# Upward feed-forward products of a second pass, written as seven block products for eight

## The chip, the core and the metric

One core of one Trainium2 chip runs the whole kernel. The metric is device time in microseconds (us), the median of several runs. TensorE does the matrix products, VectorE and ScalarE work on 128 partitions side by side, GpSimd does one reduction, and SyncE starts nearly all DMA transfers.

## The reference

The inputs are float32. Four batches of twelve heads, 448 positions of 64 values, go through an attention with a capped score; the result x has 4 x 448 = 1792 rows of 768. Two feed-forward layers follow, and only the second one's result is returned.

```python
x = attention(q, k, v, cap)                  # (1792, 768): tanh cap, softmax, times v
h = np.maximum(x @ w_in, 0.0)                # w_in (768, 2048)
x = h * h @ w_out                            # (2048, 768)
g = x @ w_gate                               # w_gate, w_val (768, 1536)
x = g * (1 / (1 + np.exp(-g))) * (x @ w_val) @ w_out2    # (1536, 768)
```

## The kernel before

The 768 columns of x are six blocks of 128 (KD), kept transposed: one tile holds 128 columns of one batch by its 448 rows. The feed-forward work is cut into **units**. A "1a" unit makes 128 columns of h (six blocks of contraction), a "2a" unit 128 columns of the gate or of the value, a "1b" or "2b" unit adds four blocks (FG) of the hidden layer into 128 columns of the result. `units` (L398) lists them: for each group of four hidden blocks the upward units, then six downward ones, first for layer one (4 groups), then for layer two (3 groups). That is 16 "1a", 24 "1b", 24 "2a" and 18 "2b".

The batches go through this list in two passes: pass 0 takes batches 0 and 1 (with the attention of batches 2 and 3 fitted in between its units), pass 1 takes batches 2 and 3. In a pass each unit runs for one batch and then for the other.

Every product is made in three matmuls (`unit_mm`, L497; the matmul L508): a float32 operand is split into a rounded piece and what is left of it, and high x high, high x low and low x high are added up in PSUM. One contraction block therefore costs three matmuls of 128 x 128 by 448. Splitting a weight block costs a cast on ScalarE (`w_hi`, L482) and a subtraction on VectorE (`w_lo`, L487); the same holds for x (`x_hi`, L391, `x_lo`, L395) and for the hidden layer (`g_hi`, L543, `g_lo`, L547). What comes after an upward product is on ScalarE (relu L523, square L527, tanh of the gate L531) and VectorE (L535, L539); a downward product is added to the sum on VectorE (`gather`, L555; the first group is copied on ScalarE, L553). Results are transposed on VectorE (L560) and stored from SyncE's queue (L565).

Weights arrive as 64-bit floats and are decoded in pass 0 on VectorE (L464, L466, L468), and written to DRAM; pass 1 reads them from there (L442). The attention's rows of batches 2 and 3 lie in DRAM too (`hold`, L384) and come back at the start of pass 1, twelve loads of 224 KB (`x_back`, L388).

The order of all work is made by a planner, `Plan.order` (L38): each operation has an engine, an assumed duration, a rank (when it would be due) and a list of what it needs, and buffers go round in rings. It takes the operation that can start first, and among equals the one with the lowest rank. The result is one fixed order for each engine, and engines take their queues in that order. Constants such as PACE, AHEAD, LATER, SLACK and MARGIN (L137 to L152) only move ranks and assumed delays. The instructions of SyncE's queue, loads, stores and the write-back of decoded weights, are one such order.

Of the kernel before, what the change touches and what calls it, by code (L numbers as in the profile page):

```python
# [101 lines left out]
def kernel(  # L102
# [34 lines left out]
    FIRST = [15.0, 20.6]  # L137
    LAST = [80.7, 39.3]
    STRETCH = 1.8

    AHEAD = dict(
        ld=45.5, lv=27.5, tr=4.6, cp=3.2, sc=9.4, th=-3.9, top=-8.4, par=-2.5, mp=6.1, sub=16.3,
        ex=20.4, rs=-12.2, av=30.6, rc=15.3, norm=-4.5, xh=33.0, xl=30.4,
    )
    LATER = dict(
        ld=-22.4, lv=-11.1, tr=6.7, sc=-4.9, th=11.3, top=9.7, par=19.0, sub=25.6, ex=16.7,
        tot=26.9, av=11.0, rc=4.2, norm=-13.9, xh=27.9, xl=34.2,
    )
# [262 lines left out]
    passes = [([0, 1], units(0)), ([2, 3], units(0))]  # L411
# [246 lines left out]
    PAIR = 6.33  # L658
# [193 lines left out]
```

## Time and profile before

| | |
|---|---|
| median of 3 runs | 1242.69 us (1242.67 to 1242.75) |
| the profiled execution's own time | 1251.49 us |
| its span, first to last instruction | 1249.4 us |
| TensorE busy, share of the span | 98% |
| VectorE, ScalarE, GpSimd | 65%, 42%, 6% |
| mean granted TensorE clock | 0.996 of full speed |

The profile is of one execution. Busy times are sums over instructions, and idle time is put down to what ended it. Pass 0 with the attention lasts to 736 us of the span, pass 1 from there to 1243 us, and the last 6 us are the store of the result. The table's shares are means over both passes, so they must not be read as those of either.

### The profile page before, as it was taken

The page shows a single profiled execution, that of the slowest core. Times are in us where ns is not written, and L with a number is a line of the kernel's source. Part 1 is how long each engine was busy: PE and PEld are TensorE (multiplying, and loading weights), DVE is VectorE, ACT ScalarE, POOL GpSimd, SP SyncE. Part 2 cuts the span into 40 slices and gives each one's busy share as a digit, 9 for nine tenths or more (in the row PEclk, how much of TensorE's full clock was granted, in tenths as well). Part 3 has the DMA queues.
Part 4 walks back from the last instruction along what each step waited for, and adds up shares of the span by engine and source line. Part 5 has one row for each costly group of instructions (what it writes and reads, how often), then busy time and mean ns, then how long its engine had stood idle before and what let it go on. Part 6 is the DMA issues. An engine that isn't in the chain of part 4 may idle for free.

```text
span 1249.4 us, 16191 instructions
## 1 busy us (share of the span) xinstructions
PE 1229.2 (98%) x6292; PEld 999.8 (80%) x6292; DVE 814.4 (65%) x1261; ACT 528.4 (42%) x788; POOL 75.9 (6%) x31
## 2 busy tenths in 40 slices
PE   8989999999999999999999999999999999999997
PEld 5334477887887787788788889999999999999997
DVE  5999888878888988888898863133335432334334
ACT  5988754626354443534234335333334223221220
POOL 2222110100010000011001000000000000000000
PEclk9999999999999999999999999999999999999999
DMA  7352057365463664753664783111212112112004
GB/s 139 68 135 67 16 153 202 119 171 153 123 175 116 176 170 118 200 159 115 155 187 133 205 217 93 57 47 55 56 60 61 41 55 65 47 51 63 26 1 89
DMA packets 214428, 135.54 MB, mean 108 GB/s; under 512 B 144816, under 2 KB 193360, under 8 KB 214352
## 3 DMA queue, kind: packets, MB, share of 16 engines
q1 hardware_dynamic: 212496, 134.28, 39.6%
q8 instruction: 49, 0.80, 0.3%
q10 hardware_dynamic: 1856, 0.23, 0.1%
q14 instruction: 27, 0.22, 0.1%
HBM read 99.48 MB, written 35.00 MB: 108 GB/s over the span
## 4 chain that ended last, share of the span: by engine, by line
PE 89%; DVE 7%; DMA 2%; issue 1%; ACT 1%; POOL 0%; SPq 0%; DVEq 0%; ACTq 0%
PE ff L508 77%; PE av L345 5%; PE sc L259 5%; DVE mx L278 1%; PE rs L309 1%; DVE te L296 1%; DVE tt L296 1%; DVE x L395 1%; DMA out_dram<-ob 0%; PE rs L329 0%; DVE acc L555 0%; DMA wx<-w 0%; DVE wx L468 0%; DVE wx L466 0%; DVE wp L487 0%
## 5 line engine op out<-in xcount | busy, mean ns | idle before, releaser
L508 PE MATMUL ff<-x,wp 128*128 128x448 f32 x2880 | 600.9, 368 | 0.5 <-DVE x L395 0.5
L508 PEld LDWEIGHTS ff<-x,wp 128*128 128x128 f32 x2880 | 538.0, 188 | 69.2 <-issue 19.2
L508 PE MATMUL ff<-g,wp 128*128 128x448 f32 x2016 | 418.7, 367 | 0.0
L508 PEld LDWEIGHTS ff<-g,wp 128*128 128x128 f32 x2016 | 377.4, 188 | 43.3 <-issue 9.4
L482 ACT CAST wp<-wx 128x768 fp32r<-128x768 f32 (+1 forms) x164 | 118.5, 723 | 223.8 <-PE ff L508 112.7
L487 DVE TENSOR_TENSOR wp<-wx,wp 128x512 fp32r<-128x512 f32 (+1 forms) x164 | 134.2, 820 | 64.6 <-ACT wp L482 63.5
L547 DVE TENSOR_TENSOR g<-gg,g 128x448 fp32r<-128x448 f32 x112 | 70.2, 627 | 110.2 <-ACT g L543 109.9
L555 DVE TENSOR_TENSOR acc<-ff,acc 128x448 f32<-128x448 f32 x120 | 74.6, 622 | 76.3 <-PE ff L508 75.0
L283 POOL PARTITION_ALL_REDUCE mr<-mx x24 | 75.1, 3131 | 582.9 <-DVE mx L278 547.3
L543 ACT CAST g<-gg 128x448 fp32r<-128x448 f32 x112 | 63.4, 566 | 85.5 <-DVE gg L539 83.1
L259 PE MATMUL sc<-kT 64*112 64x448 f32 x384 | 88.6, 571 | 1.9 <-DVE xs L381 1.3
L535 DVE SCALAR_TENSOR_TENSOR sg<-th,ff 128x448 f32<-128x448 f32 x48 | 29.8, 620 | 76.7 <-ACT th L531 76.7
L300 ACT ACTIVATE tt<-tt,capt 112x896 f32<-112x896 f32 x60 | 62.5, 1045 | 23.4 <-DVE tt L296 23.2
L523 ACT ACTIVATE r<-ff 128x448 f32<-128x448 f32 x64 | 34.8, 544 | 87.8 <-PE ff L508 87.8
L531 ACT ACTIVATE th<-ff 128x448 f32<-128x448 f32 x48 | 26.2, 546 | 106.5 <-PE ff L508 106.2
L466 DVE SCALAR_TENSOR_TENSOR wx<-wr,wx 128x512 int32<-128x512 int32 (+1 forms) x82 | 68.5, 836 | 1.8
L468 DVE SCALAR_TENSOR_TENSOR wx<-wr,wx 128x512 int32<-128x512 int32 (+1 forms) x82 | 66.9, 816 | 1.1
L259 PEld LDWEIGHTS sc<-kT 64*112 64x112 f32 x384 | 31.5, 175 | 44.0 <-issue 26.3
L539 DVE SCALAR_TENSOR_TENSOR gg<-ff,sg 128x448 f32<-128x448 f32 x48 | 29.9, 624 | 51.6 <-PE ff L508 51.4
L272 ACT ACTIVATE tt<-sc,capt 112x896 f32<-112x896 f32 x48 | 46.2, 1006 | 33.5 <-PE sc L259 33.4
L553 ACT COPY acc<-ff 128x448 f32<-128x448 f32 x48 | 25.6, 533 | 65.4 <-PE ff L508 65.2
L296 DVE TENSOR_TENSOR tt<-tt,mr 112x896 f32<-112x896 f32 x48 | 51.8, 1084 | 0.0
(57 smaller groups left out, 703.8 us busy)
## 6 DMA issues: line engine op xcount, KB each, us to landing
w<-wx SPq DMA_DIRECT2D x40, 384.0 KB, 2.7
wx<-w SPq DMA_DIRECT2D x40, 384.0 KB, 3.1
wr<-in_moe_w_in_dram SPq DMA_DIRECT2D x16, 768.0 KB, 5.8
wr<-in_moe_w_out_dram SPq DMA_DIRECT2D x24, 512.0 KB, 4.1
w<-wx SPq DMA_DIRECT2D x42, 256.0 KB, 2.3
wx<-w SPq DMA_DIRECT2D x42, 256.0 KB, 2.6
wr<-in_moe_w_gate_dram SPq DMA_DIRECT2D x12, 768.0 KB, 5.1
wr<-in_moe_w_val_dram SPq DMA_DIRECT2D x12, 768.0 KB, 5.0
```

Source lines behind the costliest of these rows:

```text
L259: PE.matmul(to, d["kT"][r, 0, c * CP : (c + 1) * CP], d["kT"][r, 1], start=True, stop=True)
L283: G.partition_all_reduce(d["m"].rearrange("p j s -> p (j s)"), d["mx"].rearrange("p j s -> p (j s)"), CP, bass_isa.ReduceOp.max)
L296: V.tensor_tensor(d["t", c], d["t", c], d["m"], ALU.subtract)
L300: A.activation(t, t, AF.Exp, scale=c_abs)
L466: V.scalar_tensor_tensor(x, hi, -0x40000000, x, ALU.bitwise_and, ALU.bitwise_or)
L468: V.scalar_tensor_tensor(x, lo, 29, x, ALU.logical_shift_right, ALU.bitwise_or)
L482: A.copy(hl[:, 0], raws[ps, i])
L487: V.tensor_tensor(hl[:, 1], raws[ps, i], f32(hl[:, 0]), ALU.subtract)
L508: PE.matmul(ffn_ps[i, b][:, :S], hl[:, h, c], x[:, t], start=(c == 0 and s == 0), stop=(c == cnt(u) - 1 and s == 2),)
L543: A.copy(g_t[b, f][:, 0], tmp_t[i, b])
L547: V.tensor_tensor(g[:, 1], tmp_t.pop((i, b)), f32(g[:, 0]), ALU.subtract)
L555: V.tensor_tensor(acc, pt, acc, ALU.add)
```

## The change

Pass 1's upward products of both batches are made together. With x of batch 2 and batch 3 as two columns of a block matrix, the contraction's first and last three blocks as its two halves, and two weight columns (two neighbouring hidden blocks in layer one, gate and value of the same block in layer two) as the two rows, one unit is a 2 x 2 by 2 x 2 block product, which Strassen's scheme (in Winograd's form) makes in seven block products for eight. Each block product is three contraction blocks, nine matmuls. Eight units "1s" and twelve "2s" take the place of 16 "1a" and 24 "2a".

- Four sums and differences of weights for each unit (`w_sum`) are split into pieces, as the plain columns were. Both columns of a unit are loaded ahead of it (`reload`).
- Four sums of x (T1 to T4, `x_sum`) are made for each of three block pairs, once for layer one and once for layer two, and split too; nine of these tiles live in attention buffers (`HOME`). In layer one the rows of x are loaded for T1, T2 and T3 (`BACK`) and again for the parts used as they are and for T4 (`AGAIN`): eighteen loads for twelve.
- The seven products are added up on VectorE (`s_sum`), after a copy of the first on ScalarE. Relu, square, tanh, gate and value then work from SBUF.
- Pass 1's downward units run batch 3 before batch 2, the first two of a group in an order of their own (`some`), and the last group of layer one takes its columns in the order 0, 3, 1, 4, 2, 5.
- Pass 0's output tiles use the attention's `kq` buffers, not `mx`. Rank constants of pass 0 and of the attention have other values.

The core of the diff:

```diff
-    FIRST = [15.0, 20.6]
-    LAST = [80.7, 39.3]
-    STRETCH = 1.8
+    FIRST = [15.0, 5]
+    LAST = [80.7, 37.1]
+    STRETCH = 2.1
+    EARLIER = 16.02
+    LEAD = 21.46
+    BYC = 6.75
+    BYK = 1.6
...
+    PACE = 7.11
+    SLACK = 2.39
+    MARGIN = 0.21
+    DECODE = 77.14
...
-    passes = [([0, 1], units(0)), ([2, 3], units(0))]
...
+    def pairs():
+        seq = []
+        for n, ff, k2 in (("1", FF1, 1), ("2", FF2, 2)):
+            for g in range(ff // FG):
+                seq += [(n + "s", f) for f in range(FG * g, FG * g + FG, 2 // k2)]
+                mixed = n == "1" and g == ff // FG - 1
+                seq += [(n + "b", g, e) for e in ((0, 3, 1, 4, 2, 5) if mixed else range(KD))]
+        return seq
+    passes = [([0, 1], units(0)), ([2, 3], pairs())]
...
-    def load_tag(i):
...
+    def column(u, h):
+        return ("1a", u[1] + h, 0) if u[0] == "1s" else ("2a", u[1], h)
...
+    def load_tag(h):
+        return ("kq", 2) if h else ("wx", 2)
+    def reload(i, h):
+        u = passes[1][1][i]
+        key = column(u, h) if seven(u) else u
+        n = cnt(key)
+        h = h if seven(u) else i % 2
+        tag, bufs = load_tag(h)
+        raws[1, i, h] = (ap if h else fp).tile([P, n, 128], F32, tag=tag, bufs=bufs, name="wx")
+        nc.sync.dma_start(raws[1, i, h], scratch[key])
...
+    def piece_tag(n):
+        return ("wr", 2) if n % 6 > 3 else ("wp", WP)
+    def piece(key, n):
+        tag, bufs = piece_tag(n) if key[0] else ("wp", WP)
+        t = pieces[key] = fp.tile([P, 2, KD, 128], F32R, tag=tag, bufs=bufs, name="wp")
+        return t
...
+    def w_sum(i, k):
+        r0, r1 = raws[1, i, 0], raws[1, i, 1]
+        if k == 3:
+            V.tensor_tensor(r1[:, :3], r0[:, :3], r1[:, :3], ALU.subtract)
+            return
+        if k == 1:
+            for n in (1, 2):
+                s_t[i, n] = fp.tile([P, 3, 128], F32, tag="sg", bufs=2, name="ws")
+        elif k == 4:
+            s_t[i, k] = ap.tile([P, 3, 128], F32, tag="v", bufs=2, name="ws")
+        t = s_t[i, k]
+        if k == 1:
+            V.tensor_tensor(t, r1[:, :3], r1[:, 3:], ALU.add)
+        elif k == 2:
+            V.tensor_tensor(t, s_t[i, 1], r0[:, :3], ALU.subtract)
+        else:
+            V.tensor_tensor(t, r0[:, 3:], s_t[i, 2], ALU.subtract)
...
+    def s_hi(i, k, n):
+        t = piece((1, i, k), n)
+        for src, r in parts(i, k):
+            A.copy(t[:, 0, r], src)
+    def s_lo(i, k):
+        t = pieces[1, i, k]
+        for src, r in parts(i, k):
+            V.tensor_tensor(t[:, 1, r], src, f32(t[:, 0, r]), ALU.subtract)
...
+    SUMS = {"T1": ("12", "11"), "T2": ("22", "T1"), "T3": ("22", "12"), "T4": ("21", "T2")}
+    KINDS = ("11", "21", "T2", "T1", "22", "T3", "T4")
+    HOME = {("T1", 0): "t", ("T1", 1): "t", ("T1", 2): "t", ("T2", 0): "t", ("T2", 1): "kT", ("T2", 2): "kT",
+            ("T3", 0): "m", ("T3", 1): "mx", ("T3", 2): "mx"}
+    RING = {"t": TBUF, "kT": 2, "m": 1, "mx": 2}
+    for c in range(3):
+        xo["11", c], xo["21", c], xo["T4", c], xo["22", c] = xbuf[0][c], xbuf[0][c + 3], xbuf[1][c], xbuf[1][c + 3]
...
+    def x_sum(kind, c):
+        one, two = SUMS[kind]
+        t = fp.tile([P, S], F32, tag="xt", bufs=2, name="xt")
+        if kind == "T4":
+            V.tensor_tensor(t, xf[one, c], f32(xo[two, c][:, 0]), ALU.subtract)
+            V.tensor_tensor(t, t, f32(xo[two, c][:, 1]), ALU.subtract)
+        else:
+            V.tensor_tensor(t, xf[one, c], xf[two, c], ALU.subtract)
+        xf[kind, c] = t
...
+    SEVEN = ((0, 0, "11", "f0", 0), (0, 1, "21", "f0", 0), (2, 1, "T2", "s", 0), (2, 0, "T1", "s", 1),
+             (3, 0, "22", "f1", 0), (1, 0, "T3", "a", 0), (1, 1, "T4", "a", 1))
...
+    def s_mm(i, p, c):
+        k, half, kind, tag, side = SEVEN[p]
+        if c == 0:
+            if tag in ("f0", "f1"):
+                bank[i, p] = ps_f.tile([P, 512], F32, tag=tag, name="ff")[:, :S]
+            else:
+                if side == 0:
+                    bank[i, tag] = (ps_s if tag == "s" else ps_a).tile([P, 2, 512], F32, tag=tag, name="ff")
+                bank[i, p] = bank[i, tag][:, side, :S]
+        hl, x = pieces[1, i, k], xo[kind, c]
+        for n, (h, t) in enumerate(((0, 0), (0, 1), (1, 0))):
+            PE.matmul(bank[i, p], hl[:, h, 3 * half + c], x[:, t], start=(c == 0 and n == 0), stop=(c == 2 and n == 2))
...
+    def s_sum(i, what):
+        if what == "p1":
+            u_t[i, 1] = ap.tile([P, S], F32, tag="xs", bufs=2, name="u1")
+            A.copy(u_t[i, 1], bank[i, 0])
+        elif what == "u":
+            u_t[i, "u"] = ap.tile([P, S], F32, tag="xs", bufs=2, name="u2")
+            V.tensor_tensor(u_t[i, "u"], bank[i, 2], u_t[i, 1], ALU.add)
+        elif what == "v":
+            u_t[i, "v"] = ap.tile([P, S], F32, tag="r", name="u5")
+            V.tensor_tensor(u_t[i, "v"], bank[i, 3], u_t[i, "u"], ALU.add)
+        elif what == "w":
+            V.tensor_tensor(u_t[i, "u"], bank[i, 5], u_t[i, "u"], ALU.add)
+        else:
+            t = c_t[i, what] = fp.tile([P, S], F32, tag="r", bufs=2, name="cs")
+            n, u = {"11": (1, 1), "12": (4, "v"), "22": (5, "v"), "21": (6, "u")}[what]
+            V.tensor_tensor(t, bank[i, n], u_t[i, u], ALU.add)
+    PLACE = {"11": (0, 2), "12": (0, 3), "21": (1, 2), "22": (1, 3)}
...
+    BACK = (("12", "xs", 2, ("T1", "T3")), ("11", "r", 1, ("T1",)), ("22", "v", 2, ("T2", "T3")))
+    AGAIN = (("11", "r", 1), ("21", "xs", 2), ("22", "v", 2))
...
+            at = start_t[1, units7["12"[stage - 1]][0], 2] - 24 + BYC * c
...
+            free_x = [("mm", 0, gone, b, x) for b in range(2) for x in (c, c + 3)]
...
+                for n, (kind, tag, bufs, to) in enumerate(BACK):
+                    b, p = x_where(kind, c)
+                    add(("xr", kind, c), "SP", (0.4, 0.6), at + n - EARLIER, x_back, (kind, c, tag, bufs),
+                        [("hold", b * KD + p), ("norm", B * KD - 1)], [("rb" if tag == "r" else tag, bufs, [("xt", 1, t, c) for t in to])])
+                for n, (kind, tag, bufs) in enumerate(AGAIN):
+                    b, p = x_where(kind, c)
+                    add(("xw", kind, c), "SP", (0.4, 0.6), at + n, x_back, (kind, c, tag, bufs), [("hold", b * KD + p), ("xt", 1, "T3", 2)],
+                        [("rb" if tag == "r" else tag, bufs, [("xo", 1, kind, c)] + [("xt", 1, "T4", c)] * (kind == "21"))])
...
+                early = EARLIER * (stage == 1 and (kind, c) in HOME)
+                add(("xi", stage, kind, c), "ACT", ACT1, at + 5 + BYK * n - early, high, (kind, c), deps, ring)
+                add(("xo", stage, kind, c), "DVE", DVE1, at + 6 + BYK * n - early, o_lo, (kind, c), [("xi", stage, kind, c)])
...
+    def plan_seven(i, t, prev):
+        u = passes[1][1][i]
+        stage = int(u[0][0])
+        f = u[1]
+        for p, (y, _, kind, tag, side) in enumerate(SEVEN):
+            for c in range(3):
+                deps = [("xo", stage, kind, c)]
+                if c:
+                    deps.append(("sm", i, p, c - 1))
+                else:
+                    deps.append(("wl", 1, i, y))
+                    deps += [("sm", i, p - 1, 2)] if p else [prev] if prev else []
+                ring = []
+                if c == 0 and side == 0:
+                    rel = {0: [("sp1", i)], 1: [("s11", i)], 2: [("su", i), ("sv", i)], 4: [("s12", i)], 5: [("s22", i), ("sw", i), ("s21", i)]}[p]
+                    ring = [(tag, 2 if tag in ("f0", "f1") else 1, rel)]
+                add(("sm", i, p, c), "PE", MM3, t + MM3 * (3 * p + c), s_mm, (i, p, c), deps, ring, MARGIN)
+        at = lambda p: t + 3 * MM3 * (p + 1)
...
+        for what, p in (("11", 1), ("12", 4), ("22", 5), ("21", 6)):
+            x = PLACE[what]
+            f, b = u[1] + x[0] * (stage == 1), x[1]
+            used = [("mm", 1, m, b, f % FG) for m, w in enumerate(passes[1][1]) if w[0] == u[0][0] + "b" and w[1] == f // FG]
+            K = lambda name, w=what: (name, i, w)
+            hi, lo = ("gh", b, u[0][0], f), ("gl", b, u[0][0], f)
+            e = at(p) + 0.6
+            if stage == 1:
+                add(K("crl"), "ACT", ACT1, e, c_relu, (i, what), [(f"s{what}", i)])
+                add(K("csq"), "ACT", ACT1, e + 0.5, c_square, (i, what), [K("crl")], [("gg", 2, [lo])])
+            elif x[0] == 0:
+                add(K("cth"), "ACT", ACT1, e, c_tanh, (i, what), [(f"s{what}", i)], [("gg", 2, [lo])])
+                add(K("cgm"), "DVE", DVE1, e + 0.5, c_gate, (i, what), [K("cth")])
+                continue
+            else:
+                add(K("cva"), "DVE", DVE1, e, c_value, (i, what), [(f"s{what}", i), K("cgm", f"1{what[1]}")])
+            add(hi, "ACT", ACT1, e + 1.0, c_hi, (i, what, f, b), [K("csq" if stage == 1 else "cva")], [("g", GB, used)])
+            add(lo, "DVE", DVE1, e + 1.6, c_lo, (i, what, f, b), [hi])
...
+                one = [x for x in range(i, i + KD)]
+                some = [(one[0], y, x) for y in (3, 2) for x in range(3)] + [(one[0], 3, 3)]
+                some += [(one[1], 3, x) for x in range(FG)] + [(one[0], 2, 3)]
+                some += [(one[1], 2, x) for x in range(FG)]
+                some += [(m, y, x) for m in one[2:] for y in (3, 2) for x in range(FG)]
...
-            ob_t[b, m // 2] = ap.tile([P, TB, 2, 32], F32, tag="mx", bufs=2, name="ob")
+            ob_t[b, m // 2] = ap.tile([P, TB, 2, 32], F32, tag="mx" if b > 1 else "kq", bufs=2, name="ob")
```

## Rows read from the trace of the kernel before

**Rows 1.** The page, part 1: busy time, share of the span and instructions of each engine.

```profile
PE 1229.2 (98%) x6292; PEld 999.8 (80%) x6292; DVE 814.4 (65%) x1261; ACT 528.4 (42%) x788; POOL 75.9 (6%) x31
```

**Rows 2.** Busy time by stretch: window, its length, each engine, clock, DMA share, GB/s.

```profile
600.00:700.00 100.00, 100.00 (x501) 80.92 (x498) 88.78 (x141) 33.66 (x46) 6.29 (x2) 1.00 0.57 161
...
700.00:740.00 40.00, 39.56 (x196) 36.32 (x194) 32.17 (x56) 12.28 (x21) 0.00 (x0) 1.00 0.80 215
740.00:860.00 120.00, 119.92 (x580) 108.96 (x581) 37.69 (x56) 48.59 (x86) 0.00 (x0) 1.00 0.28 82
```

**Rows 3.** The chain of waits, its longest piece: start, length, what.

```profile
740.08 502.89 PE ff L508 x2432
```

**Rows 4.** TensorE's waits from 700 us on, and its timeline before that chain.

```profile
PE ff L508 <- DVE x L395: 0.5, 1, 0.5
...
736.15 3.41 PE L508 MATMUL ff<-x,wp 128*128 128x448 f32 x16
```

**Rows 5.** Groups by line and shape, VectorE: count, busy us, mean ns, idle before.

```profile
L487 DVE TENSOR_TENSOR wp<-wx,wp 128x768 fp32r<-128x768 f32 x80 | 76.1, 953 | 48.7 <-ACT wp L482 48.0
L555 DVE TENSOR_TENSOR acc<-ff,acc 128x448 f32<-128x448 f32 x120 | 74.6, 622 | 76.3 <-PE ff L508 75.0
L547 DVE TENSOR_TENSOR g<-gg,g 128x448 fp32r<-128x448 f32 x112 | 70.2, 627 | 110.2 <-ACT g L543 109.9
L487 DVE TENSOR_TENSOR wp<-wx,wp 128x512 fp32r<-128x512 f32 x84 | 58.2, 693 | 15.8 <-ACT wp L482 15.5
L539 DVE SCALAR_TENSOR_TENSOR gg<-ff,sg 128x448 f32<-128x448 f32 x48 | 29.9, 624 | 51.6 <-PE ff L508 51.4
L395 DVE TENSOR_TENSOR x<-xr,x 128x448 fp32r<-128x448 f32 x12 | 7.3, 607 | 1.5 <-ACT x L391 1.5
```

**Rows 6.** The same view, ScalarE.

```profile
L482 ACT CAST wp<-wx 128x768 fp32r<-128x768 f32 x80 | 66.7, 834 | 131.8 <-PE ff L508 71.4 <-DVE wx L468 58.3 <-DMA wx<-w 2.1
L543 ACT CAST g<-gg 128x448 fp32r<-128x448 f32 x112 | 63.4, 566 | 85.5 <-DVE gg L539 83.1 <-PE av L345 0.2
L482 ACT CAST wp<-wx 128x512 fp32r<-128x512 f32 x84 | 51.9, 618 | 92.0 <-DVE wx L468 47.3 <-PE ff L508 41.4 <-DMA wx<-w 3.3
L527 ACT ACTIVATE gg<-r 128x448 f32<-128x448 f32 x64 | 37.0, 578 | 2.0
L523 ACT ACTIVATE r<-ff 128x448 f32<-128x448 f32 x64 | 34.8, 544 | 87.8 <-PE ff L508 87.8
```

**Rows 7.** VectorE's timeline where it is full: start, length, what.

```profile
412.70 0.62 DVE L395 TENSOR_TENSOR x<-acc,x 128x448 fp32r<-128x448 f32 x1
413.23 0.55 DVE L464 TENSOR_SCALAR wx<-wr 128x768 int32<-128x768 int32 x1
```

**Rows 8.** Busy time around pass 0's change of layer, and TensorE's timeline there.

```profile
412.00:425.00 13.00, 13.00 (x66) 12.05 (x65) 12.97 (x20) 6.57 (x10) 0.00 (x0) 1.00 0.80 202
425.00:438.00 13.00, 11.21 (x60) 7.41 (x58) 12.65 (x23) 3.74 (x5) 0.00 (x0) 1.00 0.44 134
...
429.48 0.59 PE L329 MATMUL rs<-sm,ones 112*32 112x224 f32 x8 [0.94 <-DVE sm L322]
...
438.45 1.76 PE L259 MATMUL sc<-kT 64*112 64x448 f32 x8 [1.30 <-DVE xs L381]
```

**Rows 9.** Before pass 1: busy time, and the costliest VectorE group there.

```profile
698.80:736.30 37.50, 37.50 (x187) 34.76 (x186) 30.77 (x55) 10.48 (x18) 0.00 (x0) 1.00 0.79 207
...
L560 DVE STREAM_TRANSPOSE ob<-acc 128x448 f32<-128x448 f32 x11 | 7.1, 645 | 3.5 <-DMA out_dram<-ob 3.2 <-DVE acc L555 0.2
```

**Rows 10.** The same stretch: SyncE's queue, and DMA issues (count, size, us to landing).

```profile
699.69 0.56 SPq L384 DMA_DIRECT2D xhold<-xs  x1
...
715.79 5.81 SPq L565 DMA_DIRECT2D out_dram<-ob  x8
...
xr<-xhold SPq DMA_DIRECT2D x12, 224.0 KB, 3.3
```

More of the change, by code (lines that the diff above doesn't have):

```diff
@@ L419, in ups, with seven @@
         return u[0] in ("1a", "2a")
+    def seven(u):
+        return u[0][1] == "s"
     def last(u):
@@ L550, in gather @@
         pt = ffn_ps.pop((i, b))[:, :S]
+        if first and e % 2 == 0:
+            acc_t.pop((b, e // 2), None)
         acc = acc_slice(b, e)
@@ L662 @@
     for ps, (bs, seq) in enumerate(passes):
-        order = [(i, b) for i in range(NB) for b in bs]
+        order = [(i, b) for i, u in enumerate(seq) for b in bs[:: -1 if ps else 1] if b == bs[0] or not seven(u)]
         if ps == 0:
             order = [(i, b) for b in bs for i in range(NPRE)] + order[NPRE * len(bs) :]
-        lens = [MM3 * cnt(seq[i]) for i, _ in order]
+        lens = [MM3 * (21 if seven(seq[i]) else cnt(seq[i])) for i, _ in order]
         heads, spent, at = 0, 0.0, t
@@ L697 @@
     for ps, (bs, seq) in enumerate(passes):
-        for i in range(NB):
-            u, n, use = seq[i], cnt(seq[i]), users[ps, i]
+        turn = 0
+        for i, u in enumerate(seq):
+            n, use = cnt(u), users[ps, i]
             at = start_t[ps, i, use[0]]
@@ L722 @@
[L722 to L736 removed]
+                at -= LEAD
@@ new lines @@
+                for h in range(1 + seven(u)):
+                    key = column(u, h) if seven(u) else u
+                    hh = h if seven(u) else i % 2
+                    tag, bufs = load_tag(hh)
+                    rel = [("wl", 1, i, h), *[("ss", i, k) for k in (2, 3, 4)]] if seven(u) else [("wl", 1, i)]
+                    add(("w", 1, i, h), "SP", (0.4, 1.2 if seven(u) or big else 0.8), at + h, reload, (i, h),
+                        [("ws", passes[0][1].index(key))] + [("norm", B * KD - 1)] * (hh == 1) + [("w", 1, i, 0)] * h
+                        + [("w", 0, NB - 1)] + ([("w", 1, i - 1, int(seven(seq[i - 1])))] if i else []), [(tag, bufs, rel)])
@@ new lines @@
+            add(("wh", ps, i), "ACT", 0.83 if big else 0.6, at + 7, w_hi, (ps, i, turn), [src],
+                [(*(piece_tag(turn) if ps else ("wp", WP)), done)])
+            add(("wl", ps, i), "DVE", 0.95 if big else 0.69, at + 8, w_lo, (ps, i), [("wh", ps, i)])
+            turn += 1
+    PART = {x[2]: p for p, x in enumerate(SEVEN)}
+    units7 = {n: [i for i, u in enumerate(passes[1][1]) if u[0] == n + "s"] for n in "12"}
+    gone = max(i for i, u in enumerate(passes[0][1]) if u[0] == "2a")
@@ L737 @@
+    for ps, (bs, seq) in enumerate(passes):
+        prev, before, when = None, {}, {}
         for ps_, i, b, t in [s for s in steps if s[0] == ps]:
             u, n = seq[i], cnt(seq[i])
+            if seven(u):
+                prev = plan_seven(i, t, prev)
+                continue
+            if ps and (i, b, 0) not in when:
+                one = [x for x in range(i, i + KD)]
[3 more added lines that the diff above has]
+                some += [(m, y, x) for m in one[2:] for y in (3, 2) for x in range(FG)]
+                for x in some:
+                    before[x] = prev
+                    prev = ("mm", 1, *x)
+                    when[x] = t + MM3 * some.index(x)
@@ L753 @@
                     deps.append(("xl", b * KD + KD - 1))
-                if c == 0 and prev and not ahead:
+                if c == 0 and prev and not ahead and ps == 0:
                     deps.append(prev)
```

190 lines of the change are left out of this document (125 added, 65 removed).

## The prediction

> **What bounds the kernel now.** I read the shares of the engines first: TensorE is busy for 98% of the span, VectorE for 65%, ScalarE for 42% [rows 1]. Those are means over two different passes, so the busy time by stretch came next. Late in pass 0 TensorE has no gap in 100 us although VectorE is busy for 88.78 of them; in pass 1 TensorE is as full and VectorE is busy for 37.69 of 120 us [rows 2]. The chain of waits then says what sets the end: from 740.08 us one unbroken piece of 502.89 us, 2432 matmuls [rows 3]. The reader is to see that nothing but matmuls stands in it. TensorE's waits agree: from 700 us on it waits once, for 0.5 us, at the start of pass 1 [rows 4]. So in pass 1 a matmul less is its time less, as long as VectorE, two thirds free there, stays ahead.
>
> **The matmuls removed.** An old pair of upward units took 2 units x 2 batches x 6 blocks x 3 = 72 matmuls; a new unit takes 7 products x 3 blocks x 3 = 63. Over 20 units that is 180 fewer. 502.89 / 2432 = 206.8 ns each [rows 3], as before the same shape with the same kind of weight load, so **37.2 us** go, all of it on the path. A new unit lasts 63 x 0.2068 = 13.03 us, a product 1.86 us, a contraction block 0.62 us.
>
> **VectorE in the upward stretches.** An instruction of 384 columns isn't in the trace; between 693 ns for 512 and 953 ns for 768 [rows 5] the slope is 130 ns per 128 columns, which gives an estimate of 0.56 us. Per unit: four weight sums, 4 x 0.56 = 2.25 us; residues of the four pieces, 2 x 0.953 + 3 x 0.56 = 3.60; seven sums of products, 7 x 0.622 = 4.35. Layer one adds four residues of h, 4 x 0.627 = 2.51: **12.7 us**. Layer two adds two gates, two values and two residues, some 6 x 0.624 = 3.74: **13.9 us**, more than the 13.03 us of its matmuls. Two rows lower this. Where VectorE is full, independent instructions start closer together than they last: one of 0.62 us is followed after 0.53 us [rows 7]. At 0.08 us less for each of 22 instructions the unit is 12.1 us. And the six downward units behind each group need only 6 x 0.693 + 12 x 0.622 = 11.6 us of VectorE in 144 x 0.2068 = 29.8 us. A whole group of layer two, four units and six downward ones, is 4 x 13.9 + 11.6 = 67.4 us of VectorE in 81.9 us of TensorE, 82%; of layer one 2 x 12.7 + 11.6 = 37.0 in 55.8, 66%. Pass 0 holds a full TensorE at 88.78% [rows 2]. Six pieces of weights fit in the rings and a unit uses four, so VectorE can enter a group with about a unit and a half of weight work done ahead, 7 us, against a deficit of 4 x 0.9 = 3.6 us at full durations. I take **0 us** for all upward stretches; bounds 0 and 12 x 0.9 = 10.9 us (nothing carried over).
>
> The Trainium skill, page "VectorE: DVE Perf Modes", section "The DRAIN you can't avoid", says that after each VectorE instruction the next does not start until the pipe is empty, and advises a low instruction count; the same place adds that an instruction which is not held may start earlier. By the first half the upper bound would be the sum; the starts 0.53 us apart in this trace side with the second half.
>
> **ScalarE.** Casts of the pieces: 2 x 0.834 and three of 384 columns at an estimated 0.51 (slope between 618 and 834 ns), 3.2 us; the copy of the first product, some 0.54; in layer one 4 x (0.544 + 0.578 + 0.566) = 6.75 us [rows 6]. That is 10.5 us in 13.03: free, and what hides it is the matmuls. Its steps follow each other with VectorE's, so a late VectorE makes them late too.
>
> **From upward to downward** (seven times). The last block of h is ready after sum, relu, square, cast and residue, 0.62 + 0.54 + 0.58 + 0.57 + 0.63 = 2.9 us behind the last product; the new order of the first two downward units puts eleven blocks, 6.8 us, before its first use. 0 us; if VectorE were four microseconds behind, it would begin to cost.
>
> **The start of pass 1** is where I expect a price. Until 736.3 us VectorE is busy for 30.77 of 37.5 us, 7.1 of them transposes of pass 0's output [rows 9], which nothing on TensorE waits for soon. By the start of the seventh product, 11.2 us later, the change wants more: nine sums T1 to T3, 5.6 us; T4, six instructions, 3.7; 12 further residues of x, 7.3 at 0.607 [rows 5]; the first unit's weights, 5.0 beyond the one piece in the row; four product sums, 2.5; a last gather, 0.6. That is 24.7 us in 6.7 + 11.2 = 17.9 free ones: 6.8 us too much, or nothing if the transposes go behind, or starts overlap as in [rows 7]. The nearest row to an overfull VectorE at such a seam is pass 0's change of layer: VectorE at 12.97 of 13 us, and TensorE lost 0.94 + 1.30 = 2.2 us [rows 8].
> The loads are the other side. Block 11 goes through one buffer, six times in a row: three times for T1, three times again. A round is a load (3.3 us to land [rows 10]) plus a sum, or a cast and a residue: 3 x 3.9 + 3 x 4.5 = 25 us from the last attention row, 699.7 [rows 10], to 725, while the first product needs it whole by 737.5. But SyncE's queue stands for 5.81 us in eight output stores there [rows 10]; two such turns in the way use up the margin of 12.5 us. DMA is 80% busy in that stretch [rows 2], and six more loads come in. Bounds: 0 us and 11 us (four of the rounds each behind eight stores, less the margin). I take **3 us**, near [rows 8], in place of the old 0.5 us wait.
>
> **The change of layer in pass 1.** The last gathered column needs gather, cast and residue, 1.8 us, and the first use comes 5 blocks, 3.1 us, later; with sums of x queued on VectorE I take **1 us**, bounds 0 and 4 (the residues of one block of all seven kinds, 7 x 0.6).
>
> **Pass 0** gets other ranks, nothing else. Its units, decodes and attention instructions are the same; the 2.2 us of [rows 8] may go or come again: 0, bounds -2.2 and +2.2. The tail is the same gather, transpose and store.
>
> **Sum.** Against the profiled execution's own span: 1249.4 - 37.2 - 0.5 + 3 + 1 = 1215.7 us. The runs' median is 1242.69 / 1249.4 = 0.9946 of that span (the execution itself took 1251.49), so 1215.7 x 0.9946 = **1209 us**.
>
> **Rivals.**
> *Layer two is paced by VectorE* (0.12). Durations count in full and the rings carry nothing over: + 10.9 us. For it: 13.9 against 13.03 us. Against: [rows 7], 82% over a group. 1226.6 x 0.9946 = 1220 us.
> *The loads at the start of pass 1 are late* (0.09): 11 us for 3, 1223.7 in the span, 1217 us. For it: the single buffer and the store-blocked queue. In pass 0 a wait of 0.94 us left the granted clock at 1.00 [rows 8]; a longer wait may not. The Trainium skill, "TensorE: Matmul & The Clock Gate", section "Why this matters for your kernels", says that a long enough gap between matmuls returns the clock to half; no row here has such a gap in mid-kernel.
> *Slower: VectorE in the upward stretches, with gaps of its own* (0.05). Its queue is in order and its sums wait in turn for products and ScalarE; if it gets no fuller than the 88.8% of late pass 0 and nothing is carried over, a unit lasts 12.7 / 0.888 = 14.3 and 13.9 / 0.888 = 15.7 us: 8 x 1.3 + 12 x 2.65 = 42 us lost, 1249.4 - 37.7 + 4 + 42 = 1257.7, 1251 us. It decides once VectorE stays below about 92% in those stretches. Against: it reached 99% in [rows 8].
> *No gain* (0.04): every product begins late, 140 products x 0.27 us eat 37.2 us. Products alternate over eight PSUM banks and are emptied in one or two instructions, so I see no cause.
>
> **Numbers.** Forecast 0.70, with its own range 1203 (all seams free, pass 0 better by 2.2) to 1216 (seams at 7 and 4 us). The rivals at 1220 and 1217 are taken in, so 1202 to 1222; outside lie the last two and half of the forecast's tails. Measurement tells about 0.2%, 2.5 us, from nothing. Faster 0.91, within 0.2% 0.04, slower 0.05.
>
> **What would show it.** Right: matmuls of pass 1 at 207 ns, 2268 of them, one long piece in the chain after a wait of a few microseconds near 740 us, VectorE at 85 to 95% in layer two's upward stretches, TensorE's waits there under 1 us a unit. Wrong: TensorE waiting for weight residues or product sums unit by unit; a gap over 6 us before pass 1 ending on a load of x; pass 0 ending more than 3 us off 736 us.

## The result, and the profile after

| us | before | changed |
|---|---|---|
| median, range | 1242.68 (1242.44 to 1242.75), 4 runs | 1254.99 (1251.19 to 1256.74), 4 runs |
| the profiled execution's time, its span | 1251.49, 1249.4 | 1251.19, 1249.1 |

The changed kernel is about 1% slower: ratio 1.0095, 95% interval 1.0069 to 1.0122, against a forecast of 1209 us. The two profiled spans agree by chance. The profiled execution of before ran pass 1's matmuls at 206.8 ns [rows 3]; the first experiment traces one that ran them at 202.8, and the traces of after are best read beside that one.

The page of after, part 1, and of its costliest groups the larger one of pass 1's upward matmuls (count, busy us, mean ns, idle before and what ended most of it), against [rows 1]:

```profile
PE 1196.1 (96%) x6112; PEld 965.8 (77%) x6112; DVE 980.9 (79%) x1589; ACT 577.6 (46%) x886; POOL 73.3 (6%) x31
...
L612 PE MATMUL ff<-x,wp 128*128 128x448 f32 x720 | 165.3, 376 | 24.8 <-DVE cs L631 10.0
```

The 180 matmuls are gone (6112 for 6292), and TensorE has become idle. Its waits after (us in total, times, the longest), where [rows 4] had 0.5 us once:

```profile
PE ff L612 <- DVE cs L631: 10.0, 14, 0.7
PE ff L612 <- ACT x L589: 7.8, 4, 3.7
PE ff L612 <- DVE u L622: 5.7, 8, 0.7
PE ff L612 <- DVE u L627: 4.3, 6, 0.7
PE ff L682 <- DVE acc L731: 2.1, 1, 2.1
PE ff L612 <- DVE x L593: 1.8, 2, 0.9
PE ff L612 <- ACT u L619: 0.9, 1, 0.9
```

There are two sorts. Twenty-eight waits of 0.7 us, 20.0 in all, end on sums of products (L622, L627, L631); the rest are a few long ones. Busy time by stretch says where each lies (columns as in [rows 2]):

```profile
400.00:700.00 300.00, 300.00 (x1500) 246.50 (x1499) 261.57 (x396) 115.83 (x160) 19.61 (x7) 1.00 0.55 153
720.00:740.00 20.00, 11.69 (x39) 8.04 (x37) 18.21 (x34) 9.38 (x18) 0.00 (x0) 0.79 0.66 192
740.00:760.00 20.00, 19.07 (x85) 17.39 (x85) 16.14 (x30) 7.39 (x13) 0.00 (x0) 0.87 0.34 93
800.00:950.00 150.00, 138.54 (x664) 123.11 (x663) 84.36 (x140) 63.81 (x112) 0.00 (x0) 1.00 0.18 52
950.00:1000.00 50.00, 44.81 (x201) 39.10 (x200) 43.01 (x78) 24.44 (x44) 0.00 (x0) 0.93 0.19 56
```

Pass 0 has no gap. The start of pass 1 (720 to 760) and the change of layer (950 to 1000) are seams with a busy VectorE (18.21 of 20 us at the worst, 43.01 of 50), an idle TensorE and a lower granted clock. Between them, 800 to 950, VectorE is only 56% busy and TensorE still loses 11.5 us. There the one long piece of [rows 3] has become many; from the chain of waits (start, length, what):

```profile
802.33 6.71 PE ff L612 x33
...
809.74 5.15 PE ff L612 x24
...
817.18 6.97 PE ff L612 x33
...
833.78 29.19 PE ff L682 x144
```

Within a product, not between two, the piece breaks off. One unit in the timeline, TensorE and then VectorE (start, length, what, and the wait ahead of it):

```profile
809.74 0.88 PE L612 MATMUL ff<-xo,wp 128*128 128x448 f32 x3 [0.72 <-DVE u L622]
...
815.59 0.88 PE L612 MATMUL ff<-x,wp 128*128 128x448 f32 x3 [0.72 <-DVE cs L631]
...
817.18 0.47 PE L612 MATMUL ff<-x,wp 128*128 128x448 f32 x1 [0.72 <-DVE u L627]
```

```profile
809.06 0.62 DVE L622 TENSOR_TENSOR u<-ff,u 128x448 f32<-128x448 f32 x1 [1.42 <-PE ff L612]
...
814.92 0.62 DVE L631 TENSOR_TENSOR cs<-ff,u 128x448 f32<-128x448 f32 x1 [1.09 <-PE ff L612]
...
816.51 0.62 DVE L627 TENSOR_TENSOR u<-ff,u 128x448 f32<-128x448 f32 x1 [0.97 <-PE ff L612]
```

VectorE waits for TensorE, not the reverse: it is idle for 1.42 us, then sums for 0.62 us, and TensorE stands for just those 0.62 us and 0.1 around them. The code says why. `SEVEN` puts products 3 and 4 into the two sides of one PSUM tile "s" and products 6 and 7 into the two sides of "a". The sum of product 3 was placed behind the first block or the first two of product 4, which writes the other side of its tile: it waits for them, and the next block waits for it. The two sums of product 6 stand between blocks of product 7 in the same way. Three such places a unit, at most, are 0.72 us of idle time each; the pieces between them also last longer than their matmuls do elsewhere (5.15 us for 24, 215 ns each, for some 202).

The Trainium skill, "PSUM — Partial Sum Buffer", section "PSUM bank collisions raise a hardware error", asks that readers and writers be kept apart by bank, and its section "The four PSUM rules" gives a bank 512 float32 values; by that the two sides, 512 values each, are two banks and need no order between them. The trace shows the order kept all the same, for the tile as a whole. What two engines on the two sides at once would do, no run here tried.

### The profile page after: what moved, and what is told of

Its sections match the earlier page's. It is cut to its first block, busy times and chain, and to the rows that moved or that the text cites. A ratio compares the mean times of both kernels' runs of the same rounds, so it can differ in the third digit from the quotient of the medians.

```text
span 1249.1 us, 16273 instructions
## 1 busy us (share of the span) xinstructions
PE 1196.1 (96%) x6112; PEld 965.8 (77%) x6112; DVE 980.9 (79%) x1589; ACT 577.6 (46%) x886; POOL 73.3 (6%) x31
## 4 chain that ended last, share of the span: by engine, by line
PE 88%; DVE 8%; DMA 1%; issue 1%; ACT 1%; SPq 0%; POOL 0%; DVEq 0%
PE ff L682 55%; PE ff L612 21%; PE av L349 5%; PE sc L263 5%; DVE mx L282 1%; PE rs L313 1%; DVE te L300 1%; DVE cs L631 1%; DMA out_dram<-ob 1%; PE rs L333 0%; DVE acc L731 0%; DVE u L622 0%; DVE x L593 0%; DVE xt L582 0%; DVE u L627 0%
## 5 line engine op out<-in xcount | busy, mean ns | idle before, releaser
L682 PE MATMUL ff<-x,wp 128*128 128x448 f32 x1440 | 301.9, 368 | 0.0
L682 PEld LDWEIGHTS ff<-x,wp 128*128 128x128 f32 x1440 | 267.8, 188 | 41.4 <-issue 19.2
L612 PE MATMUL ff<-x,wp 128*128 128x448 f32 x720 | 165.3, 376 | 24.8 <-DVE cs L631 10.0
L612 PEld LDWEIGHTS ff<-x,wp 128*128 128x128 f32 x720 | 135.6, 192 | 46.8 <-DVE cs L631 15.3
L508 ACT CAST wp<-wx 128x512 fp32r<-128x512 f32 (+1 forms) x124 | 85.0, 687 | 124.3 <-DVE wx L490 79.3
L612 PE MATMUL ff<-xo,wp 128*128 128x448 f32 x540 | 120.6, 372 | 5.7 <-DVE u L622 5.7
L612 PEld LDWEIGHTS ff<-xo,wp 128*128 128x128 f32 x540 | 102.7, 191 | 17.4 <-DVE u L622 8.7
L513 DVE TENSOR_TENSOR wp<-wx,wp 128x512 fp32r<-128x512 f32 (+1 forms) x124 | 95.8, 776 | 12.2 <-ACT wp L508 11.8
L631 DVE TENSOR_TENSOR cs<-ff,u 128x448 f32<-128x448 f32 x80 | 49.6, 621 | 37.2 <-PE ff L612 36.7
L547 ACT CAST wp<-wx 128x768 fp32r<-128x768 f32 x40 | 33.4, 836 | 65.4 <-PE ff L682 46.3
L552 DVE TENSOR_TENSOR wp<-wx,wp 128x768 fp32r<-128x768 f32 x40 | 38.1, 953 | 25.2 <-ACT wp L547 25.1
L547 ACT CAST wp<-ws 128x384 fp32r<-128x384 f32 x60 | 29.0, 512 | 59.6 <-PE ff L612 30.2
```

Of the source, the lines that this page charges most:

```text
L508: A.copy(piece((ps, i), n)[:, 0, :m], raws[1, i, i % 2] if ps else raws[0, i])
L513: V.tensor_tensor(hl[:, 1, :m], raws[1, i, i % 2] if ps else raws[0, i], f32(hl[:, 0, :m]), ALU.subtract)
L547: A.copy(t[:, 0, r], src)
L612: PE.matmul(bank[i, p], hl[:, h, 3 * half + c], x[:, t], start=(c == 0 and n == 0), stop=(c == 2 and n == 2))
L682: PE.matmul(ffn_ps[i, b][:, :S], hl[:, h, c], x[:, t], start=(c == 0 and s == 0), stop=(c == cnt(u) - 1 and s == 2),)
```

## The experiments

The expectations name theories by letters: A, that products sharing a tile hold each other up; and of the seams, C, that loads of x are late, D, that VectorE has too much to do there, E, that the lower clock costs the time. All ratios below are to the kernel before, run beside it on the same chip; its medians there were 1241.6 to 1243.0 us, so times from different chips stand on nearly the same base.

**1. before_again.** The kernel before, unchanged, to have its usual execution in a trace.

> The kernel before, unchanged. If an execution of it always takes what the runs showed: 1242.7 us, within 0.2%, with a span about 2 us less. If the profiled execution shown at first (1251.5 us) is as common: values of both sizes in its runs.

Median 1241.85 us (1238.18 to 1252.38, 10 runs), 0.998 [0.995, 1.0014], span 1238.6. One run of the ten was as long as the execution profiled at first. Its longest piece of the chain, and a stretch of it:

```profile
696.26 535.88 PE ff L508 x2643
```

```profile
740.00:860.00 120.00, 120.00 (x594) 111.23 (x593) 37.24 (x55) 49.81 (x87) 0.00 (x0) 1.00 0.26 80
```

535.88 / 2643 = 202.8 ns, for 206.8 in [rows 3], at a granted clock of 1.00 in both. At 202.7 ns, the 180 matmuls are 36.5 us, and a change that did only this would have a span of 1202.1 us. After's matmuls ran at this rate too (a downward stretch of 144 took 29.19 us, 202.7 ns). So the loss to be explained is 1249.1 - 1202.1 = 47 us by spans.

**2. changed_again.** The changed kernel, unchanged, run again.

> The changed kernel as it is, on the same chip as the other two: 1251 to 1257 us as in its four runs, 0.5 to 1.3% over the kernel before.

1255.12 us (1250.63 to 1258.62, 5 runs), 1.0104 [1.0069, 1.0139]: the result repeats.

**3. split_sides.** Product 4 goes to tile "a" and product 6 to "s", so that no two neighbours share a tile (the list of sums that free each tile, not shown, follows).

```diff
-    ... (2, 1, "T2", "s", 0), (2, 0, "T1", "s", 1),
-    (3, 0, "22", "f1", 0), (1, 0, "T3", "a", 0), (1, 1, "T4", "a", 1))
+    ... (2, 1, "T2", "s", 0), (2, 0, "T1", "a", 0),
+    (3, 0, "22", "f1", 0), (1, 0, "T3", "s", 1), (1, 1, "T4", "a", 1))
```

> Only the PSUM places of four products change: products 3 and 6 share one two-bank tile, 4 and 7 the other, so that no product is summed on VectorE while TensorE writes the same tile. Theory A (VectorE reading one half of a tile holds back TensorE's next matmuls into its other half): the waits of 0.7 us on the product sums, 20.0 us in all in the changed kernel's profile (10.0 + 5.7 + 4.3), go; a few us may come back at the two seams: 1251 to 1255 less 20, so 1230 to 1237 us. Theory B (VectorE is behind in the upward stretches, and the waits are its lateness): VectorE has the same work, so the time stays within 5 us of the changed kernel's.

1229.54 us (1226.57 to 1234.33), 0.9903 [0.9874, 0.9931], 25 us less than the changed kernel, with no instruction less.

**4. sum_later.** Tiles as in the changed kernel; the sums of products 3 and 6 are made to wait for the whole of products 4 and 7.

```diff
-        add(("su", i), ..., [("sp1", i), ("sm", i, 2, 2)], ...)
+        add(("su", i), ..., [("sp1", i), ("sm", i, 3, 2)], ...)
-        add(("sw", i), ..., [("sv", i), ("sm", i, 5, 2)])
+        add(("sw", i), ..., [("sv", i), ("sm", i, 6, 2)])
-            add((f"s{what}", i), ..., [(d, i), ("sm", i, p, 2)], ...)
+            add((f"s{what}", i), ..., [(d, i), ("sm", i, 6 if p == 5 else p, 2)], ...)
```

> Products stay where they are; the sums of products 3 and 6 are put behind products 4 and 7, so that VectorE reads a tile only when TensorE has finished both halves. Theory A: the 20.0 us of waits go, some 0.7 us for each of 7 changes to downward units come in their place, as the last sums are 1.9 us later: 1235 to 1242 us. Theory B: sums that start later make a late VectorE later: slower than the changed kernel, over 1255 us.

1229.43 us (1228.82 to 1235.86), 0.9915 [0.9882, 0.9947]: as good as the split, better than expected of it. A sum that comes later cost nothing here. Busy time in the upward stretches:

```profile
800.00:950.00 150.00, 150.00 (x739) 138.24 (x738) 91.08 (x153) 70.87 (x125) 0.00 (x0) 1.00 0.19 60
1000.00:1200.00 200.00, 200.00 (x989) 185.32 (x988) 150.46 (x263) 72.95 (x130) 0.00 (x0) 1.00 0.18 56
```

TensorE has no gap in either, and VectorE does not set the pace of layer two: 150.46 of 200 us. Two edits with nothing in common but the sharing give the same 25 us, so theory A is shown.

That the two spans differ by 20.8 us (1249.1 - 1228.3), close to the 20.0 us of waits, is chance. A cleaner measure counts matmuls: the time from the 3700th matmul of a trace (late in pass 0) to the 4150th, the 4850th, the 5150th and the last, less as many times 202.7 ns. It gives what each part of pass 1 loses; from the 3700th matmul on all are of one shape.

| us lost in | start of pass 1 | layer one | change of layer | layer two |
|---|---|---|---|---|
| after | 17.3 | 16.8 | 7.6 | 10.1 |
| changed_again | 17.8 | 16.9 | 8.1 | 10.0 |
| split_sides | 18.4 | 0.0 | 10.4 | 0.0 |
| sum_later | 18.3 | 0.4 | 7.4 | 0.0 |

The sharing cost after 16.8 + 10.1 = 26.9 us in the two layers, for the 27 waits that stand there: 1 us each, 0.72 of it idle. The seams of split_sides are 3.9 us longer, and it reached the 3700th matmul 2.2 us later (703.9 for 701.7), with a granted clock of 0.93 for 1.00 from 50 to 100 us. That leaves the 20.8.

What is left is in the seams: 18.4 + 10.4 = 28.8 us in split_sides. Busy time there, and TensorE's first products of pass 1:

```profile
735.00:745.00 10.00, 4.36 (x9) 2.76 (x10) 9.44 (x19) 3.75 (x8) 0.00 (x0) 0.54 0.45 134
...
950.00:1000.00 50.00, 45.18 (x204) 39.79 (x203) 44.91 (x82) 21.54 (x41) 0.00 (x0) 0.93 0.11 36
970.00:980.00 10.00, 5.99 (x23) 4.15 (x22) 9.97 (x20) 5.16 (x10) 0.00 (x0) 0.91 0.00 1
980.00:985.00 5.00, 5.00 (x15) 4.38 (x15) 5.00 (x9) 1.87 (x3) 0.00 (x0) 0.50 0.37 120
```

```profile
737.70 1.77 PE L612 MATMUL ff<-x,wp 128*128 128x448 f32 x3 [3.87 <-ACT x L589]
741.51 0.74 PE L612 MATMUL ff<-x,wp 128*128 128x448 f32 x1 [2.04 <-ACT x L589]
```

Waits at the first seam add up to 11.1 us, at the second to 4.8. Where they stand the granted clock falls to 0.54 and behind them to 0.50, the lower of the engine's two levels (1.2 GHz); from 980 to 985 us 15 matmuls took 5.0 us, which at 202 ns are 3.0. What sets this was tried in several ways.

**5. load_once** (on split_sides). Block 11, which went through one buffer six times, is loaded once into buffers that stay. Only the two tables of loads are shown.

```diff
-    BACK = (("12", "xs", 2, ("T1", "T3")), ("11", "r", 1, ("T1",)), ...)
-    AGAIN = (("11", "r", 1), ("21", "xs", 2), ("22", "v", 2))
+    BACK = (("12", "xs", 2, ("T1", "T3")), ("11", "g", GB, ()), ...)
+    AGAIN = (("21", "xs", 2), ("22", "v", 2))
```

> Built on split_sides. Block 11 of x is loaded once, early, into two free tiles of the hidden layer's ring, and one block 21 beside it: 15 loads for 18, and no chain of loads through one buffer. Theory C (the wait at the start of pass 1 is the loads': a load of x stands behind stores and another load in SyncE's queue): most of the 9.3 us that TensorE stands still between 724 and 743 us goes, and with it the slow clock behind it: 10 to 14 us less than split_sides, 1215 to 1220 us. Theory D (VectorE has too much to do there, and the loads only pass its lateness on): the wait moves to another step, within 3 us of split_sides' 1229.5.

1230.18 us (1227.19 to 1231.84), 0.9888 [0.9838, 0.9939]: no change. TensorE's longest waits now:

```profile
PE ff L619 <- DVE x L600: 6.1, 2, 5.0
PE ff L689 <- DVE acc L738: 3.6, 2, 2.6
PE ff L619 <- DVE wp L552: 2.7, 1, 2.7
```

In the changed kernel the chain of waits passes through a load of x at this seam:

```profile
731.62 3.38 DMA xr<-xhold
735.02 0.57 ACT x L589
```

With the load gone TensorE waits about as long for VectorE, and the time is the same; the start of pass 1 loses 18.5 us for 18.4. From 726 us to TensorE's next long piece (742 us) the chain of waits now holds no load. Theory C falls. VectorE is not only busy there: its queue is in order, and in load_once it stood for 3.9 us before two transposes of output whose buffers were still being stored.

```profile
DVE ob L743 <- DMA out_dram<-ob: 3.9, 2, 2.2
```

**6. sums_twice** (on split_sides). Every sum of x is made twice, 0.6 us of VectorE for each of 18.

```diff
-            V.tensor_tensor(t, xf[one, c], xf[two, c], ALU.subtract)
+            for _ in range(2):
+                V.tensor_tensor(t, xf[one, c], xf[two, c], ALU.subtract)
```

> Built on split_sides. Each of the sums T1, T2 and T3 of x is made twice on VectorE, with the same result: nine more instructions, 5 us of VectorE at 0.55 each, at the start of pass 1 and nine more at its change of layer. Theory D (VectorE is the bound at both seams): 4 to 5 us more at each, 8 to 10 us in all, 1237 to 1240 us. Theory C (loads): the start of pass 1 hides it, under 2 us more there; the change of layer, with no loads of x, is not spoken of by C.

1240.23 us (1233.53 to 1242.75, 10 runs), 0.9962 [0.9933, 0.9991]: 10.7 us more for 18 x 0.6 = 10.8 us of VectorE. The change of layer shows it, beside the row of split_sides above (TensorE 41.49 for 45.18, VectorE 46.04 for 44.91):

```profile
950.00:1000.00 50.00, 41.49 (x185) 36.33 (x184) 46.04 (x83) 19.25 (x34) 0.00 (x0) 0.90 0.10 32
```

What VectorE gets to do at a seam is paid: theory D. How much of it is less sure than the medians look. In the two traces the seams lose 3.9 and 3.7 us more than in split_sides, 7.6 for the 10.8; the trace of sums_twice also has layer two's matmuls at 206.7 ns, 3.8 us more.

**7. fill** (on split_sides). Into the waits go 48 matmuls whose result nobody reads, so that TensorE is not idle. (The tile that they write is taken earlier in these two units; not shown.)

```diff
+    FILL = {0: {(0, 1): 18, (0, 2): 10, (1, 0): 4}, units7["2"][0]: {(1, 0): 4, (1, 2): 8, (2, 0): 4}}
...
+        for n in range(FILL.get(i, {}).get((p, c), 0)):
+            PE.matmul(bank[i, "s"][:, 1, :S], pieces[1, i, 0][:, 0, 0], xo["11", 0][:, 0], start=True, stop=True)
```

> Built on split_sides. 32 matmuls of no use (128 x 128 by 448, into a bank not yet in use) stand in TensorE's queue in the waits of the first unit of pass 1, 16 more in those of the first unit of layer two. Theory E (after these waits TensorE runs some 8 to 15 us at half clock, which costs some 9 us at both seams beside the waits): the granted clock stays nearer to 1.00 in 735 to 745 and 980 to 985 us of the span and the time falls by 4 to 9 us, to 1220 to 1226. If the slow clock costs nothing, since VectorE is the bound there anyway: same time within 2 us, or up to 3 us more.

1229.86 us (1227.45 to 1231.15), 0.9884 [0.9843, 0.9925]. The two stretches:

```profile
735.00:745.00 10.00, 7.85 (x34) 6.12 (x34) 9.42 (x18) 3.44 (x7) 0.00 (x0) 1.00 0.59 168
980.00:990.00 10.00, 8.83 (x41) 7.43 (x40) 8.71 (x17) 3.43 (x6) 0.00 (x0) 1.00 0.25 79
```

The clock is 1.00 in both, and the median is the same. In the trace, whose added matmuls are left out of the count, the seams lose 16.5 + 8.6 = 25.1 us for 28.8; layer one ran at 206.7 ns, 2.8 us more, which hides that. That is no less than sum_later lost at the lower clock (25.7). So the clock accounts for some 4 us of the 28.8 at most, and theory E is not the main cause: VectorE set the pace, and faster matmuls mostly waited longer.

**8. seam_order** (on load_once). The work is the same; ranks move, so that VectorE does at the seams first what TensorE needs first, and pass 0's transposes of output come 23 us later. (BYK and two constants that place layer two's sums of x move too; not shown.)

```diff
-    EARLIER = 16.02
-    LEAD = 21.46
-    BYC = 6.75
+    EARLIER = 13.71
+    LEAD = 15.44
+    BYC = 5.33
...
-                        add(("otr", b, e), "DVE", DVE1, end + 0.6, ...
+                        add(("otr", b, e), "DVE", DVE1, end + 0.6 + 23.39 * (ps == 0), ...
```

> Built on load_once; only ranks differ: pass 0's output transposes are put off by 23 us, and the order in which sums and residues of x and first weights stand in VectorE's queue at the two seams is another. VectorE's work is the same. If the order at the seams costs most of the 26 us that split_sides has over matmuls alone: 5 to 8 us less than load_once, 1222 to 1225 us. If it is the amount of VectorE work whatever its order: within 3 us of 1230.

1216.53 us (1212.62 to 1219.46), 0.9793 [0.9751, 0.9835]: 13.6 us less than load_once, about twice what was expected. In the traces the seams lose 7.3 + 5.2 us for 18.5 + 10.1. At the start of pass 1, against 11.00 and 17.67 us of TensorE and VectorE in load_once (720 to 740) at a clock of 0.87:

```profile
720.00:740.00 20.00, 16.16 (x76) 13.60 (x74) 19.77 (x37) 9.81 (x18) 0.00 (x0) 1.00 0.45 136
740.00:760.00 20.00, 18.33 (x87) 16.06 (x88) 19.83 (x37) 11.87 (x23) 0.00 (x0) 1.00 0.37 104
```

VectorE is now as good as full for 40 us, waits for no store there, and the clock stays at 1.00.

**9. transposes_early** (on seam_order). The transposes go back to where they were; the other ranks stay.

```diff
-                        add(("otr", b, e), "DVE", DVE1, end + 0.6 + 23.39 * (ps == 0), ...
+                        add(("otr", b, e), "DVE", DVE1, end + 0.6, ...
```

> seam_order with the output transposes of pass 0 back at their old rank; the other ranks stay. Theory F (what seam_order won is the 7 us of VectorE transposes taken out of the start of pass 1): back to within 3 us of load_once's 1230. If the order of sums, residues and weights won it: 1216 to 1219 us as in seam_order.

1224.39 us (1220.25 to 1231.45), 0.9886 [0.9849, 0.9922], between the two kernels and as no theory had it. By medians the transposes are 7.9 of the 13.6 us. The two profiled spans differ by only 0.9 (1218.2 and 1217.3), but the trace of seam_order reached the 3700th matmul 3.3 us later and has layer two's matmuls at 206.7 ns, 3.8 us more. By parts the start of pass 1 loses 15.5 us here for 7.3 and the change of layer 5.1 for 5.2: the transposes are 8.2 us, all at the start, as the medians have it. VectorE's wait for a store is back too (2.2 us). Of the 16.1 us that seam_order won at the seams over load_once, the other ranks are then 3.0 at the start and some 5 at the change of layer.

**10. order_sums_twice** (on seam_order). The doubled sums again.

> seam_order with the sums T1, T2, T3 made twice, 5 us of VectorE more at each seam. If VectorE's work still sets both seams in the better order: 8 to 10 us over seam_order, 1224 to 1227 us. If the better order has left slack there: under 3 us more.

1227.71 us (1224.98 to 1233.13), 0.9899 [0.9866, 0.9932], 11.2 us more, as in sums_twice. The seams lose 13.1 + 10.3 us for 7.3 + 5.2, 10.9 more for 10.8 us of work: in the better order VectorE's work is paid one for one.

**11. gpsimd_sums** (on seam_order). The four sums of weights of a unit go to GpSimd (one is shown).

```diff
-            V.tensor_tensor(t, r1[:, :3], r1[:, 3:], ALU.add)
+            G.tensor_tensor(t, r1[:, :3], r1[:, 3:], ALU.add)
...
-                        add(("ss", i, y), "DVE", 0.53, at + 5 + y, w_sum, (i, y), d, rings.get(y, []))
+                        add(("ss", i, y), "POOL", 1.0, at + 5 + y, w_sum, (i, y), d, rings.get(y, []))
```

> Built on seam_order, with the four weight sums of each unit on GpSimd, which has nothing else to do in pass 1: VectorE loses 2.2 us of each unit, 4 to 7 us at each seam. Theory D (amount of VectorE work at the seams): 5 to 10 us less than seam_order. Against it stands that GpSimd may be slow or may hold VectorE up: its sums then come late to the first product of a unit, or VectorE's instructions of two SBUF operands get longer than 0.62 us: same time or slower.

1220.89 us (1219.01 to 1222.79), 0.9829 [0.9788, 0.987]: 4.4 us more, a miss; the start of pass 1 loses 11.2 us for 7.3. One group of the sums on GpSimd (whole run), and two groups on VectorE (800 to 1200 us), by line and shape:

```profile
L531 POOL TENSOR_TENSOR ws<-wx 128x384 f32<-128x384 f32 x20 | 25.0, 1251 | 380.2 <-DMA wx<-w 138.7 <-DVE wp L552 90.9 <-DVE xo L600 51.4
...
L657 DVE SCALAR_TENSOR_TENSOR gg<-gg,cs 128x448 f32<-128x448 f32 x24 | 17.3, 721 | 2.1 <-ACT gg L653 2.1
...
L638 DVE TENSOR_TENSOR cs<-ff,u 128x448 f32<-128x448 f32 x72 | 44.7, 621 | 31.0 <-PE ff L619 29.9
```

Such a sum takes GpSimd 1.25 us, for some 0.55 on VectorE, and a unit's weights are ready later: TensorE waited once for 8.7 us on a weight residue (L552). VectorE is slowed as well: L657, which reads two operands from SBUF, took 617 ns in seam_order and 721 here, while L638, with one operand from PSUM, stayed at 621 (622). The Trainium skill, "SBUF — State Buffer", section "Who interferes with whom", says that VectorE's second pair of ports is GpSimd's only one, held by one of them at a time; these rows agree (GpSimd worked for 74.6 of the 400 us, so only some of the 24 can have met it).

**12. seam_order_2** (on seam_order). Ranks again (EARLIER 14.93, LEAD 15.54, transposes 38 us later).

> seam_order with the transposes put off by 38 us for 23 and two ranks moved by a microsecond. VectorE's work at the start of pass 1 gets less by the transposes that still stood before 745 us, some 2 to 4 of twelve: 1 to 3 us less than seam_order, 1213 to 1216 us; the same if they had stood behind the first unit already.

1215.49 us (1212.84 to 1217.88), 0.9794 [0.9769, 0.982]. It is no better than seam_order beyond what runs of one kernel differ by; both are 2.1% faster than the kernel before and some 3.1% faster than the change.

## Why the prediction was wrong

- **Matmuls removed, 37.2 us:** right in number, 180, all on the path. At 202.7 ns they are 36.5. Worked from before_again, 1238.6 - 36.5 + 4, and 2.1 us from span to time, the forecast would have been 1208 us; that the profiled execution was one at 206.8 ns did no harm.
- **"No gain: every product begins late" (0.04):** here the prediction failed. It gave the rival 0.27 us a product, just what would eat the gain, and dismissed it with "Products alternate over eight PSUM banks and are emptied in one or two instructions, so I see no cause". Four of the seven products share two tiles in pairs, `SEVEN` says so in the diff, and 27 places of 1 us cost the two layers 26.9 us where 0 stood in the sum; one more lies in a seam. Fewer products are late than the rival has it, and each by more. The mark set for it, TensorE waiting for product sums unit by unit, is what the waits show.
- **Start of pass 1, 3 us:** 17.3 us, outside the bounds of 0 to 11. The mechanism, VectorE overfull, was right (sums_twice), the size was not. The working had 6.8 us too much for VectorE and took less because transposes could go behind; the order of the changed kernel did not put them there, and transposes_early shows 8.2 us for that. "Loads late" (0.09) was not it (load_once); that VectorE itself would stand behind the stores of output was not thought of.
- **Change of layer, 1 us:** 7.6 us in after and 10.4 in split_sides, outside the bounds of 0 to 4. VectorE was busy for 14.97 of 15 us there, 970 to 985 in split_sides. The working counted the chain behind the last gather, 1.8 us, and at most seven residues; VectorE had a full queue of sums and residues of x and of weights.
- **Upward stretches, 0 us:** as to VectorE's pace right, once the shared tiles are gone: 150.00 of 150 and 200.00 of 200 us in sum_later. VectorE reached 75% from 1000 to 1200 us where 82% was worked out for a group of layer two, so "layer two paced by VectorE" falls. An instruction of 384 columns took 0.55 us (L552: 551 ns) for an estimate of 0.56, and ScalarE's cast 0.51, as estimated.
- **Pass 0, 0 +- 2.2 us:** TensorE was full from 400 to 700, so the 2.2 us of [rows 8], which before_again has too, went. By the 3700th matmul after is 4.7 us ahead of before_again (701.7 for 706.4). Some 2 us of that are no part of the change: traces of after and of the kernels built on it reach this matmul between 701.7 and 705.7 us, and differ in the clock granted in the first 100 us (0.95 to 1.00 on average).

By parts, against before_again: -36.5 for the matmuls, -4.7 in pass 0, +26.9 for the shared tiles, +17.3 and +7.6 at the seams, +10.6 in all; the spans are 1238.6 and 1249.1. The forecast had +4 for the last three, which measured 51.8. Of load_once's 28.6 us at the seams, order won 16.1 in the trace of seam_order; that the 12.5 left are VectorE's work is shown only as far as adding to it costs one for one.

## What to carry over

Look up in which PSUM tile each product lies before trusting that products and their sums overlap: two or three waits for one short sum in a unit of seven products ate most of a real saving, and assigning neighbours to different tiles, or making the sum wait a product longer, gave it back for nothing. Work that is free on average is paid where stages meet; at such a seam add up the engine's queue up to the first use, and order it by who is waited for. To tell which of load, engine and clock sets a seam, change one of them alone: what the chain named here (a load) was not the cause. Compare traces by the time between the same two matmuls: whole spans hid or made up several microseconds here.

## What the runs showed of the hardware

- The same matmuls of pass 1 took 202.7 or 206.7 ns each, at a granted clock of 1.00 in both, and the rate can change within an execution: seam_order had 202.7 in layer one and 206.7 in layer two (3.8 us more), fill the reverse (2.8 more). Runs of the kernel before range from 1238 to 1253 us; that the longer ones are those at 206.7 ns throughout is shown for the one that was profiled alone, and why there are two rates is open.
- Filling TensorE's waits kept the granted clock at 1.00, where it had been 0.50 to 0.54; the seams lost 25.1 us for 28.8 in the traces, and the medians did not move, since VectorE, not TensorE, mostly set the pace there.
- VectorE instructions with two operands in SBUF were 17% longer on average in the kernel in which GpSimd worked beside them (L657, 617 to 721 ns); those with one operand in PSUM were not (L638, 622 and 621 ns).
